# The head of a kernel's load queues, re-ordered: two thirds of DFT tables in front, small tables behind

## The chip, the cores and the metric

The kernel runs on one core of a Trainium2 chip. The metric is the device time of one execution in microseconds (us), the median of the runs that are shown; lower is better. The chip's engines named here are TensorE (PE; its weight loads are listed apart as PEld), VectorE (DVE), ScalarE (ACT), GpSimd (POOL) and SyncE (SP). Transfers are issued by SP, ACT and POOL and are carried by 16 DMA engines. The profile calls SP's queue q1, ACT's q10 and POOL's q0.

## What is computed

Two stages in a row. The first is a global filter along the sequence: a real FFT of length 3008 over each of 8 batches of 256 channels, a product with a complex filter, and the inverse FFT. The second is a small MLP on every one of the 24064 tokens, whose activation is "snake".

```python
X = np.fft.rfft(x, axis=1)                       # x: 8 x 3008 x 256
Y = X * (filt_r + 1j * filt_i)[None]             # 1505 x 256 filter
y = np.fft.irfft(Y, n=3008, axis=1)
h = y.reshape(24064, 256) @ w_in                 # 256 x 2048
s = np.sin(alpha * h)
out = (h + s * s / (alpha + 1e-9)) @ w_out       # 2048 x 256
```

All inputs and the output are float32 in DRAM. The kernel computes in float16 with float32 sums in PSUM.

## The kernel before, in words

**The transform.** 3008 is 47 x 64, so the FFT becomes two rounds of small DFTs as matmuls. The forward way is a 47-point DFT, then, with table `wb`, the 64-point part for each of 24 residues; the result `xs` is multiplied by the filter `fri` (`product`), and the backward way is `wg` (64-point part) and then `we` (47-point part). Tables `wb`, `wg` and `wgs` are 128 x 3072 float16 and are loaded in thirds of eight residues, 1024 columns, 256 KB each.

**Batch 0 is special.** For batches 1 to 7, each re-ordering between the rounds goes through DRAM (`scr`), beside the MLP of earlier tokens. Batch 0 has nothing to hide behind, so it stays on chip: `f1_chip(k)` for k = 0 to 7 (line 173) multiplies 94 rows of x by the table `wa2`; `turn1` (line 184) transposes with the identity `ident`; `f2x`, `product` and `g_chip` (line 194, with `wg` and `wgs`) follow; `turn2` transposes back; `f3` (line 281) uses `we2` for batch 0 and `we` for the others. `f1` (line 146, with `wq`) is the first round of batches 1 to 7.

**The MLP.** 47 chunks of 512 tokens. `mlp_in` (L310) makes 16 matmul pairs a chunk, ACT takes the sine (L312), DVE squares (L317), and `mlp_out` or `fast_out` (L329, L409) multiplies by `w_out`. From the first chunk on, the work of the transforms of batches 1 to 7 is dealt into the MLP by the slots of a written plan.

**The order at the start.** The program is written under a manual schedule: each engine executes its instructions in the order of the text. What matters here, in that order:

- SP issues `wa2` (94 rows of 192 bytes), `ident` (128 rows of 256 bytes) and the first third of `wb` (128 rows of 2 KB). ACT issues `alpha_r` (16 rows of 512 bytes), `ident32` (16 rows of 64 bytes), `we2` (96 rows of 188 bytes), `wq` (128 rows of 128 bytes) and `we` (96 rows of 188 bytes).
- POOL issues x of batch 0 in four parts of two transfers, 80 and 14 rows (`load_x(0, 4)`, line 133; a row is 8 KB in DRAM and 4 KB in SBUF), then by thirds: four transfers of the filter (`load_filter`, line 535), the rest of `wb` once, a third of `wg`, a third of `wgs`; then `w_in`, x of batch 1 and `w_out`. The first filter transfer is held by `gate` until the first half of x has landed. Completion semaphores are reused in turn, eight of them for POOL's transfers, so that a POOL transfer also waits for the one eight places before it.
- PE executes `prep_alpha` (line 481: a matmul of `alpha_r` and `ident32`), then `keep_busy(8, zero)` (line 529), eight 512-column matmuls of `ident` with zeros whose result nobody reads, then the eight `f1_chip`, with two more such matmuls after every second one, and then the list of steps at line 650.

In `prep_alpha` the wait is for `alpha_r` and `ident32`; in `keep_busy` for `ident`; in `f1_chip` for a part of x and for `wa2`. PE does none of them before the one ahead.

Of the kernel before, what the change touches and what calls it, by code (L numbers as in the profile page):

```python
# [67 lines left out]
def kernel(  # L68
# [10 lines left out]
    nc = tc.nc  # L79
# [3 lines left out]
    def dram(ap, off, dims):  # L83
# [3 lines left out]
    wq_d = nc.inline_tensor(wq_np, name="wq_tbl")  # L87
    wb_d = nc.inline_tensor(wb_np, name="wb_tbl")
    wg_d = nc.inline_tensor(wg_np, name="wg_tbl")
    we_d = nc.inline_tensor(we_np, name="we_tbl")  # L90
    wa2_d = nc.inline_tensor(wa2_np, name="wa2_tbl")
    we2_d = nc.inline_tensor(we2_np, name="we2_tbl")
    wgs_d = nc.inline_tensor(wgs_np, name="wgs_tbl")
    id32_d = nc.inline_tensor(np.eye(16).astype(np.float32), name="id32_tbl")
    id_d = nc.inline_tensor(np.eye(128).astype(np.float16), name="id_tbl")
# [17 lines left out]
    wq = cpool.tile([128, 64], FP16, name="wq")  # L113
    we = cpool.tile([4 * NK, GT], FP16, name="we")
    wa2 = cpool.tile([GT, 4 * NK], FP16, name="wa2")
    we2 = cpool.tile([4 * NK, GT], FP16, name="we2")
    wb = cpool.tile([128, NK * 128], FP16, name="wb")
    wg = cpool.tile([128, NK * 128], FP16, name="wg")
# [6 lines left out]
    xt, asb, scr1, bint, xs, z, t2, gsb, scr2, gin, yt, vt, po, ot, x_dma, w_in_dma, filter_dma, swap_dma = (  # L125
        {} for _ in range(18))

    def gate(ins, earlier):

        tc.add_manual_dep(ins.ins, earlier.ins.name, mybir.DependencyInfo(  # L130
            mybir.DependencyClass.Sync, mybir.DependencyReason.DATA), reason="order of transfers")

    def load_x(b, parts=2):

        xt[b] = (xbpool if b else vpool).tile([128 if b else GT, RP, C], FP16, name="xt", tag="xb" if b else "vt")
        n = RP // parts
        for h in range(parts):
            for p0, p1, row, step in (((0, 32, 0, R), (32, MT, 32 * R, R), (64, 96, RP, R), (96, 64 + MT, 32 * R + RP, R))
                                      if b else ((0, 80, 0, RP), (80, GT, 80 * RP, RP))):
                x_dma[b, h] = nc.gpsimd.dma_start(  # L140
                    out=xt[b][p0:p1, n * h:n * h + n, :],
                    in_=dram(x, (b * S + row + n * h) * C, [[step * C, p1 - p0], [1, n * C]]))
                if b > 2 and h == p0 == 0:
                    gate(x_dma[b, 0], swap_dma[b - 1, 5])
# [170 lines left out]
    def square(g, q):  # L315
        v4 = vt[g][:, 2 * q - 2:2 * q + 2, :]
        nc.vector.tensor_tensor(out=v4, in0=v4, in1=v4, op=ALU.mult)  # L317
# [156 lines left out]
    ident = cpool.tile([128, 128], FP16, name="ident")  # L474
# [6 lines left out]
    def prep_alpha():  # L481
        ps = out_bank("psal", 0)
        nc.tensor.matmul(out=ps[:, 0, 0:16], lhsT=alpha_r, rhs=ident32, start=True, stop=True)
        nc.vector.tensor_copy(out=alpha_t, in_=ps[:, 0, 0:16])
        nc.vector.tensor_scalar(out=recip, in0=alpha_t, scalar1=1e-9, scalar2=None, op0=ALU.add)
        nc.vector.reciprocal(out=recip, in_=recip)
# [124 lines left out]
        at(8 * g + 12.5, fast_mid, g)  # L611

    with tc.manual_schedule():
        nc.sync.dma_start(out=wa2, in_=wa2_d.ap())
        nc.sync.dma_start(out=ident, in_=id_d.ap())
        nc.scalar.dma_start(out=alpha_r, in_=moe_alpha.rearrange("(a p) -> a p", p=128))
        nc.scalar.dma_start(out=ident32, in_=id32_d.ap())
        nc.scalar.dma_start(out=we2, in_=we2_d.ap())
        nc.scalar.dma_start(out=wq, in_=wq_d.ap())
        nc.scalar.dma_start(out=we, in_=we_d.ap())  # L620
        nc.sync.dma_start(out=wb[:, 0:8 * 128], in_=wb_d.ap()[:, 0:8 * 128])
        zero = spool.tile([128, 512], FP16, name="zero", tag="z")
        nc.vector.memset(zero, 0.0)
        warm = cpool.tile([128, 1], FP32, name="warm")
        nc.vector.memset(warm, 0.0)
        nc.scalar.activation(out=warm, in_=warm, func=AFT.Sin)
        load_x(0, 4)
        wgs = ginpool.tile([128, NK * 128], FP16, name="wgs", tag="gin")
        for s0 in (0, 8, 16):
            cs = slice(128 * s0, 128 * s0 + 1024)  # L630
            load_filter(s0, 8, None if s0 else x_dma[0, 1])
            if s0 == 0:
                nc.gpsimd.dma_start(out=wb[:, 8 * 128:], in_=wb_d.ap()[:, 8 * 128:])
            nc.gpsimd.dma_start(out=wg[:, cs], in_=wg_d.ap()[:, cs])
            nc.gpsimd.dma_start(out=wgs[:, cs], in_=wgs_d.ap()[:, cs])
        for h in range(2):
            hs = slice(1024 * h, 1024 * h + 1024)
            for cb in range(2):
                w_in_dma[h, cb] = nc.gpsimd.dma_start(out=w_in16[:, cb, hs],
                                                      in_=moe_w_in[128 * cb:128 * cb + 128, hs])  # L640
        a_c = vpool.tile([128, 2, NK, 128], FP16, name="a_c", tag="vt")
        prep_alpha()
        keep_busy(8, zero)
        for k in range(8):
            f1_chip(k)
            if k % 2:
                keep_busy(2 if k < 7 else 1, zero)
        bint[0] = xbpool.tile([128, NK, C], FP16, name="bint", tag="xb")
        b_c = agpool.tile([128, 2, RP, NK, 4], FP16, name="b_c", tag="ag")
        for f, *args in (  # L650
                (keep_busy, 1, zero), (turn1, 0), (turn1, 1), (turn1, 2), (f2x, 0, 0), (f2x, 0, 1),
                (keep_busy, 1, zero), (turn1, 3), (turn1, 4), (fold_filter, 0, 0, 8), (turn1, 5), (f2x, 0, 2),
                (turn1, 6), (f2x, 0, 3), (fold_filter, 1, 0, 8), (turn1, 7), (product, 0, 0, 0), (product, 0, 0, 1),
                (product, 0, 1, 0), (f2x, 0, 4), (turn1, 8), (fold_filter, 0, 8, 8), (turn1, 9), (turn1, 10),
                (f2x, 0, 5), (keep_busy, 1, zero), (product, 0, 1, 1), (f2x, 0, 6), (fold_filter, 1, 8, 8),
                (f2x, 0, 7), (turn1, 11), (keep_busy, 2, zero), (g_chip, 0, 1), (f2x, 0, 8), (g_chip, 0, 0),
                (g_chip, 1, 1), (g_chip, 1, 0), (keep_busy, 1, zero), (product, 0, 2, 0), (product, 0, 2, 1),
                (keep_busy, 2, zero), (f2x, 0, 9), (keep_busy, 2, zero), (product, 0, 3, 0), (g_chip, 2, 0),
                (g_chip, 2, 1), (product, 0, 3, 1), (f2x, 0, 10), (fold_filter, 0, 16, 8), (f2x, 0, 11),
                (product, 0, 4, 0), (g_chip, 3, 1), (fold_filter, 1, 16, 4), (g_chip, 3, 0), (keep_busy, 2, zero),  # L660
                (fold_filter, 1, 20, 4), (product, 0, 4, 1), (keep_busy, 2, zero), (product, 0, 5, 0),
                (product, 0, 5, 1), (keep_busy, 1, zero), (g_chip, 4, 0), (g_chip, 4, 1), (g_chip, 5, 1, 2, 2),
                (g_chip, 5, 0), (g_chip, 5, 1, 0, 2, False), (keep_busy, 1, zero)):
            f(*args)
        gin[0] = ginpool.tile([4 * NK, RP, C], FP16, name="gin", tag="gin")
        for j in range(4):
            turn2(j)
        load_x(1, 4)
        load_w_out(0)
        load_w_out(1)  # L670
        for i in range(4):
            if i % 2 == 0:
                keep_busy(1, zero)
            f3(i // 2, i % 2)

        for g in range(NCH):
            fast_g = g - 1 in FAST
            for q in range(8):
                if g and q == 7 and not fast_g:
                    evict_out(g - 1, 0)  # L680
                mlp_in(g, 2 * q)
                if fast_g:
                    fast_out(g - 1, 16 * q, 16 * q + 8)
                elif g:
                    mlp_out(g - 1, q, 1)
                for f, args in plan.get(16 * g + 2 * q, ()):
                    f(*args)
                mlp_in(g, 2 * q + 1)
                if fast_g:
                    fast_out(g - 1, 16 * q + 8, 16 * q + 16)  # L690
                elif g:
                    mlp_out(g - 1, q, 0)
                for f, args in plan.get(16 * g + 2 * q + 1, ()):
                    f(*args)
                if g and q == 7:
                    if not fast_g:
                        evict_out(g - 1, 1)
                    store_out(g - 1, 0, 4, (nc.sync,))
                if q % 2:
                    square(g, q)  # L700
        out_last(NCH - 1)
# [28 lines left out]
```

## Time and profile before

| | us |
|---|---|
| median of 3 runs | 796.55 |
| lowest and highest | 796.06, 796.63 |
| the profiled execution | 796.66 |
| its span in the profile | 794.9 |
| PE busy | 779.0 (98%) |
| DVE busy | 682.5 (86%) |
| ACT busy | 652.8 (82%) |
| POOL busy | 53.7 (7%) |
| granted PE clock, mean | 0.999 |

The span is what the profiler saw from the first to the last instruction; the execution's time is 1.76 us longer. In a line of the timeline the first number is the start in us from the span's start, the second the time in us that the merged instructions took, then engine, line, operation, `output<-input`, the shape and the count; the bracket tells how long the engine was idle before and what ended that. The program's names are cut at the digits: `wa` is `wa2`, `ident` is `ident` or `ident32`, `we` is `we` or `we2`, and `w_in` also `w_in16` and others. In an answer on DMA, "packets" are the descriptors that the engines worked on, and a queue's "share of 16 engines" is the summed time of its packets by 16 times the window.

### The profile page before, as it was taken

How to read it: one execution, taken by the hardware profiler on the slowest of the kernel's cores; microseconds unless marked ns; L12 is line 12 of the kernel's file. 1: busy time of each engine (PE TensorE's matmuls, PEld its weight loads, DVE VectorE, ACT ScalarE, POOL GpSimd, SP SyncE). 2: the span in 40 equal slices, each digit the busy share in tenths (PEclk: the TensorE clock that was granted, in tenths of full speed). 3: DMA queues.
4: the chain of work that ended last, by engine and by line, in shares of the span. 5: the costliest groups of instructions: out<-in, count | busy, mean ns of one | idle time of the engine just before them, and what ended most of it. 6: DMA issues, size and time to landing. Idle time of an engine off the chain costs nothing.

```text
span 794.9 us, 20782 instructions
## 1 busy us (share of the span) xinstructions
PE 779.0 (98%) x8707; PEld 567.0 (71%) x8707; DVE 682.5 (86%) x851; ACT 652.8 (82%) x1290; POOL 53.7 (7%) x104
## 2 busy tenths in 40 slices
PE   7899999999999999999999999999999999999997
PEld 4657776777677776777767777777767777777776
DVE  4786988899889989899898988899988998888783
ACT  4897988898878988798888888889888898777773
POOL 5610020002000020000200020000200000000000
PEclk9999999999999999999999999999999999999999
DMA  9977368444862466633775348623675234321122
GB/s 194 187 127 249 110 158 182 130 115 108 195 176 76 124 144 150 175 92 90 165 158 160 81 111 205 165 77 94 150 192 163 81 107 110 65 54 28 28 55 54
DMA packets 74462, 101.08 MB, mean 127 GB/s; under 512 B 7896, under 2 KB 54760, under 8 KB 72856
## 3 DMA queue, kind: packets, MB, share of 16 engines
q1 hardware_dynamic: 65136, 78.39, 36.5%
q0 software_dynamic: 8704, 21.24, 14.0%
q8 instruction: 68, 1.11, 0.6%
q14 instruction: 26, 0.21, 0.1%
q10 hardware_dynamic: 528, 0.13, 0.1%
HBM read 59.62 MB, written 46.66 MB: 134 GB/s over the span
## 4 chain that ended last, share of the span: by engine, by line
PE 84%; DMA 4%; DVE 3%; issue 0%; SPq 0%; ACT 0%; ACTq 0%; DVEq 0%
PE ph L310 37%; PE pf L409 36%; PE psy L294 2%; PE psg L266 2%; PE psx L227 2%; PE po L329 2%; PE psa L159 1%; DMA w_in<-in_moe_w_in_dram 1%; DMA bint<-scr 1%; DMA out_dram<-ot 1%; PE pe L448 1%; DMA scr<-asb 1%; DVE t L252 1%; DVE vt L317 0%; DVE w_ina L526 0%; DVE asb L163 0%
## 5 line engine op out<-in xcount | busy, mean ns | idle before, releaser
L312 ACT ACTIVATE vt<-ph 128x512 f16<-128x512 f32 x688 | 410.4, 604 | 93.4 <-PE ph L310 82.5
L310 PE MATMUL ph<-yt,w_ina 128*128 128x512 f16 x1376 | 409.6, 379 | 0.0
L317 DVE TENSOR_TENSOR vt<-vt 128x2048 f16<-128x2048 f16 x188 | 229.4, 1220 | 38.7 <-ACT vt L312 38.3
L409 PEld LDWEIGHTS <-s 128*128 128x128 f16 x2688 | 179.8, 98 | 79.6
L409 PEld LDWEIGHTS <-vt 128*128 128x128 f16 x2016 | 135.4, 98 | 59.6 <-DVE ot L423 0.4
L409 PE MATMUL pf<-tb,s 128*128 128x128 f16 x2016 | 153.6, 219 | 0.0
L423 DVE TENSOR_TENSOR ot<-pf,ot 128x512 f32<-128x512 f32 (+1 forms) x168 | 93.3, 555 | 30.6 <-PE pf L409 28.7
L310 PEld LDWEIGHTS <-w_ina 128*128 128x128 f16 x1376 | 107.1, 98 | 12.4 <-issue 9.9
L409 PE MATMUL pf<-w_out,vt 128*128 128x128 f16 x1344 | 109.3, 219 | 0.0
L360 DVE TENSOR_TENSOR s<-vt 128x2048 f16<-128x2048 f16 x84 | 102.5, 1220 | 0.9
L140 POOL DMA_DIRECT2D xt<-in_x_dram x72 | 36.8, 519 | 463.2 <-PE ph L310 267.1
L409 PEld LDWEIGHTS <-yt 128*128 128x128 f16 x672 | 47.9, 98 | 20.0
L231 ACT CAST xs<-psx 128x512 f16<-128x512 f32 x94 | 55.8, 599 | 3.7 <-PE psx L227 0.9
L409 PE MATMUL pf<-w_out,s 128*128 128x128 f16 x672 | 58.1, 219 | 0.0
L268 ACT CAST gsb<-psg 128x512 f16<-128x512 f32 x84 | 49.5, 589 | 4.5 <-PE psg L266 0.2
L360 DVE TENSOR_TENSOR s<-s,vt 128x2048 f16<-128x2048 f16 x42 | 51.3, 1222 | 0.9
L409 PE MATMUL pf<-tb,vt 128*128 128x128 f16 x672 | 51.2, 219 | 0.0
L360 DVE TENSOR_TENSOR s<-vt,s 128x2048 f16<-128x2048 f16 x42 | 51.1, 1217 | 0.0
L312 ACT ACTIVATE vt<-ph,alpha_t 128x512 f16<-128x512 f32 x64 | 43.8, 708 | 8.2 <-PE ph L310 8.1
L409 PE MATMUL pf<-m_t,yt 128*128 128x128 f16 x504 | 48.6, 219 | 0.0
L296 ACT CAST yt<-psy 128x376 f16<-128x376 f32 (+45 forms) x126 | 46.1, 366 | 1.5
L294 PE MATMUL psy<-we,gin 96*128 96x94 f16 x512 | 42.3, 204 | 0.0
(91 smaller groups left out, 702.3 us busy)
## 6 DMA issues: line engine op xcount, KB each, us to landing
scr<-asb SPq DMA_DIRECT2D x56, 192.0 KB
bint<-scr SPq DMA_DIRECT2D x21, 512.0 KB
scr<-gsb SPq DMA_DIRECT2D x21, 512.0 KB
out_dram<-ot SPq DMA_DIRECT2D x31, 320.0 KB
t<-xs SPq DMA_DIRECT2D x72, 128.0 KB
xt<-in_x_dram POOLq DMA_DIRECT2D x24, 256.0 KB, 7.1
gin<-scr SPq DMA_DIRECT2D x7, 768.0 KB
out_dram<-ot SPq DMA_DIRECT2D x16, 256.0 KB
```

What stands on the lines that cost most here:

```text
L140: x_dma[b, h] = nc.gpsimd.dma_start(out=xt[b][p0:p1, n * h:n * h + n, :], in_=dram(x, (b * S + row + n * h) * C, [[step * C, p1 - p0], [1, ...
L227: nc.tensor.matmul(out=ps[:, i, :], lhsT=wb[:, 128 * (2 * t + i):128 * (2 * t + i) + 128], rhs=bint[b][:, 2 * t + i, :], start=True, stop= ...
L231: (nc.vector.tensor_copy if b == 0 and t in (4, 5) else nc.scalar.copy)(out=xs[b, t // 2][:, t % 2 * 2:t % 2 * 2 + 2, :], in_=ps)
L268: nc.scalar.copy(out=gsb[b][:, 2 * t:2 * t + 2, :], in_=ps)
L294: nc.tensor.matmul(out=ps[:, t, :], lhsT=gin[b][:, 4 * a + t, 128 * cb:128 * cb + 128], rhs=we if b else we2, start=True, stop=True)
L296: (nc.vector.tensor_copy if G < 2 and cb == 0 else nc.scalar.copy)(out=yt[g][:, cb, :, lo:lo + n], in_=ps[:, :, 0:n])
L310: nc.tensor.matmul(out=ph, lhsT=(w_in16 if g < 4 else w_ina)[:, cb, 128 * jb:128 * jb + 128], rhs=yt[g][:, cb], start=(cb == 0), stop=(cb ...
L312: nc.scalar.activation(out=vt[g][:, jb, :], in_=ph, func=AFT.Sin, scale=alpha_t[:, jb:jb + 1] if g < 4 else 1.0)
L317: nc.vector.tensor_tensor(out=v4, in0=v4, in1=v4, op=ALU.mult)
L360: nc.vector.tensor_tensor(out=o, in0=a, in1=b, op=op)
L409: nc.tensor.matmul(out=ps[:, part, i], lhsT=a, rhs=b, start=first, stop=last)
L423: add = lambda out, in0, in1: nc.vector.tensor_tensor(out=out, in0=in0, in1=in1, op=ALU.add)
```

## The change

The first third of `wb` and the first third of `wg` become SP's first two transfers. `ident` and `wa2` move from SP to the head of ACT's queue, in this order, ahead of `alpha_r` and `ident32`. `we2`, `wq` and `we` move from ACT to SP, behind a gate on the last transfer of the second filter third (`filter_dma[8, 1]`). The first third of `wg` leaves POOL's queue; everything behind it on POOL is one place earlier. No arithmetic instruction changes or moves on PE, DVE or ACT.

```diff
     with tc.manual_schedule():
-        nc.sync.dma_start(out=wa2, in_=wa2_d.ap())
-        nc.sync.dma_start(out=ident, in_=id_d.ap())
+        nc.sync.dma_start(out=wb[:, 0:8 * 128], in_=wb_d.ap()[:, 0:8 * 128])
+        nc.sync.dma_start(out=wg[:, 0:8 * 128], in_=wg_d.ap()[:, 0:8 * 128])
+        nc.scalar.dma_start(out=ident, in_=id_d.ap())
+        nc.scalar.dma_start(out=wa2, in_=wa2_d.ap())
         nc.scalar.dma_start(out=alpha_r, in_=moe_alpha.rearrange("(a p) -> a p", p=128))
         nc.scalar.dma_start(out=ident32, in_=id32_d.ap())
-        nc.scalar.dma_start(out=we2, in_=we2_d.ap())
-        nc.scalar.dma_start(out=wq, in_=wq_d.ap())
-        nc.scalar.dma_start(out=we, in_=we_d.ap())
-        nc.sync.dma_start(out=wb[:, 0:8 * 128], in_=wb_d.ap()[:, 0:8 * 128])
...
             load_filter(s0, 8, None if s0 else x_dma[0, 1])
             if s0 == 0:
                 nc.gpsimd.dma_start(out=wb[:, 8 * 128:], in_=wb_d.ap()[:, 8 * 128:])
-            nc.gpsimd.dma_start(out=wg[:, cs], in_=wg_d.ap()[:, cs])
+            if s0:
+                nc.gpsimd.dma_start(out=wg[:, cs], in_=wg_d.ap()[:, cs])
             nc.gpsimd.dma_start(out=wgs[:, cs], in_=wgs_d.ap()[:, cs])
...
+        for tab, src in ((we2, we2_d), (wq, wq_d), (we, we_d)):
+            gate(nc.sync.dma_start(out=tab, in_=src.ap()), filter_dma[8, 1])
```

## The prediction, made before the changed kernel was run

> **What bounds the kernel now.** I read the page first.
>
> ```profile
> PE 779.0 (98%) x8707; PEld 567.0 (71%) x8707; DVE 682.5 (86%) x851; ACT 652.8 (82%) x1290; POOL 53.7 (7%) x104
> PE 84%; DMA 4%; DVE 3%; issue 0%; SPq 0%; ACT 0%; ACTq 0%; DVEq 0%
> ```
>
> PE is busy for 98% and carries 84% of the chain that ended last. So what is lost or won before the MLP starts (first `mlp_in` at 35.84) moves the end by as much: behind it PE has nearly no idle time to give back. The change touches only the first 36 us, so I read those in the timeline.
>
> ```profile
> 3.18 0.50 PEld L483 LDWEIGHTS psal<-ident,alpha_r 16*128 16x128 f32 x2 [3.18 <-DMA alpha_r<-in_moe_alpha_dram]
> 3.21 0.57 PE L483 MATMUL psal<-ident,alpha_r 16*128 16x16 f32 x2 [3.21 <-DMA ident<-id_tbl]
> 3.72 3.59 PE L533 MATMUL idle<-zero,ident 128*128 128x512 f16 x8
> ...
> 7.40 1.19 PEld L178 LDWEIGHTS <-xt 94*128 94x128 f16 x16 [1.00 <-DMA xt<-in_x_dram]
> 7.44 1.31 PE L178 MATMUL psa<-wa,xt 94*128 94x96 f16 x16
> ...
> 9.60 0.84 PE L178 MATMUL psa<-wa,xt 94*128 94x96 f16 x16 [0.42 <-DMA xt<-in_x_dram]
> ...
> 11.29 0.84 PE L178 MATMUL psa<-wa,xt 94*128 94x96 f16 x16 [0.41 <-DMA xt<-in_x_dram]
> ...
> 13.15 0.84 PE L178 MATMUL psa<-wa,xt 94*128 94x96 f16 x16 [0.59 <-DMA xt<-in_x_dram]
> ...
> 21.84 0.69 DVE L548 COPY fri<-fri 64x2048 f16<-64x2048 f16 x1 [0.49 <-DMA fri<-in_filt_r_dram]
> ```
>
> Two things to see. PE waits for the four parts of x up to 13.15; from then to 36 us DVE and ACT are the busy ones, and only one wait of theirs is for a load, the 0.49 at 21.84. And everything on PE stands behind the 16x16 matmul of L483: it starts when `alpha_r` and `ident32` have landed, the eight idle matmuls follow, and the first `f1_chip` starts 4.23 us after it (7.44 - 3.21).
>
> Then the DMA answer for four windows, in this order: 1.6 to 2.6 us (nothing was moved before 1.6), 2.6 to 3.1, 4.5 to 5.1, 6.6 to 7.4. Behind a queue's name stand its packets, their MB, and their time as a share of 16 engines.
>
> ```profile
> q1 hardware_dynamic: 240, 0.05, 23.7%
> q10 hardware_dynamic: 64, 0.01, 5.3%
> ```
> ```profile
> q0 software_dynamic: 14, 0.06, 164.0%
> ```
> ```profile
> q0 software_dynamic: 21, 0.09, 73.3%
> q1 hardware_dynamic: 22, 0.05, 22.0%
> q10 hardware_dynamic: 20, 0.00, 3.1%
> ```
> ```profile
> q0 software_dynamic: 39, 0.16, 95.8%
> q10 hardware_dynamic: 46, 0.01, 9.1%
> ```
>
> Three readings:
>
> - By 2.6 q1 has moved 240 packets: 94 rows of `wa2`, 128 of `ident`, and 18 others. Each engine that takes part in a transfer adds one small closing packet. `ident` makes 16, so `wa2` makes 2: its 94 rows (2 x 47) ran on two engines, 47 each. q10's 64 are 32 rows of `alpha_r` and `ident32` and 32 closings, so those ran on all 16.
> - Before 2.6 no packet of x moves. From 2.6 to 3.1 nothing but x moves: 14 packets, 1.64 x 16 x 0.5 / 14 = 0.94 us each.
> - After that the queues take turns packet by packet, whatever the size: 21, 22 and 20 with three queues (a turn of all three lasts 16 x 0.6 / 21 = 0.46 us), 39 to 46 with two (0.33 us). A 188-byte row of a small table gets one turn for each 8 KB row of x.
>
> **The change part by part.**
>
> *`wa2`, `alpha_r`, `ident32`.* Before, all are through by 2.6, ahead of x. After, ACT issues `ident`, `wa2`, `alpha_r`, `ident32` about 0.45 apart (its four issues before took 0.39 to 0.45), from 0.73, while SP puts 2 KB rows on every engine. A 2 KB packet takes 22.0% x 16 x 0.6 / 22 = 0.096 us. On the two engines of `wa2`, `ident` has 8 rows and a closing; taking turns with `wb`, 9 x (0.096 + 0.018) is 1.0 us from the first packets at 1.6 to 1.7 (0.018: an `ident` row, 23.7% x 16 x 1.0 / 240, rounded up). That is 2.6 to 2.7: x is there, and `wa2` has not begun. From then the pair of engines owes q10 47 + 1 turns for `wa2`, and 2 each for `alpha_r` and `ident32`, which I take to stand behind it in the same queue: 52 turns. x and its closings are only some 32 packets an engine; the filter's rows follow.
>
> When has q0 given an engine 52 turns? In the DMA answer from 2.6 to 13.5 us q0 has 831 packets, 52 for each of 16 engines. That is with 23 turns of q10 beside them (368 packets in the same window); the 29 more cost 9.1% x 16 x 0.8 / 46 = 0.025 each, 0.7 together. So `ident32` lands at 14.2 (13.5 if they cost nothing, 15.0 if x's first packets on the pair are slow ones again). From the last packet before (by 2.6) to the matmul (3.2) pass 0.6: L483 starts at 14.8, bounds 14.0 and 15.6. That is 11.6 later than 3.2.
>
> *What of it is given back.* At 14.8 + 4.23 = 19.0 all x has landed, so the waits between the four parts vanish: 0.42 + 0.41 + 0.59 = 1.42 by PE's rows, 0.88 + 0.88 + 1.05 = 2.81 by its weight loads; I take the middle, 2.1, since DVE's evictions (1.02 per part) and PE's own idle pairs (0.6) keep their pace. The 0.49 at 21.84 vanishes too (0.47 with the gap that remains); no other wait up to 36 us is for a load. Sum: 11.6 - 2.1 - 0.5 = +9.0.
>
> *First third of `wb` at the head; `wg` with it.* Needed at 15.33 and 22.27, landed by about 7 us (`wb`'s nine turns an engine by 2.7, then 0.94 and eight turns of 0.46 for `wg`'s): no gain of their own. `wg` leaves POOL's queue: 0.57 of issue and 128 x 0.096 / 16 = 0.77 of all engines, earlier for everything behind it. Only the 0.49 wait could use that, and it is counted.
>
> *`we2`, `wq`, `we` on SP behind the gate.* The gate opens when the second filter third has landed, issued at 15.38, 5.7 median to landing: about 21. SP has nothing else to issue until `scr<-asb` (its longest wait is 49.4). `we2` is needed at 34.51 and now 9 later, `wq` at 45.77: 13 us of cover; without it each us late would be a us. x loses 20 packets an engine of q10's: 4.1% of 9.8 us, 0.40, while `wg` replaces `wb` in its way.
>
> *The queues' heads.* SP's two issues take 0.43 each instead of three of 0.32 to 0.43, ACT's four instead of five: ACT's table load (3.05) comes 0.45 earlier, and ACT is idle up to 7.95. Nothing.
>
> *POOL later.* x of batch 1 waits for the PE's release of its buffer (28.09) and moves by the 9 us; `w_in` will then have landed, so the 5.1 us that POOL waits for it vanish, and no engine waits there. Its first use (45.77) moves by the same 9.
>
> The profiled execution took 796.66, 1.76 over its span, 0.11 over the median: 796.66 + 9.0 = 805.7 there, 805.6 as a median. Bounds of this case: 14.0 with 2.81 and 0.49 back gives +7.5, 804.1; 15.6 with 1.42 back gives +11.0, 807.5.
>
> **The rivals.**
>
> 1. *A turn takes many small rows.* Were a turn to take a group of `wa2`'s rows, between 8 (an engine's share of `ident`) and all 47, these need 1 to 6 turns and the whole debt is 6 to 11. 2.6 + 0.94 + 5 to 10 turns of 0.46 is 5.8 to 8.1; L483 starts at 6.4 to 8.7; 3.2 to 5.5 late, less 2.1 and 0.5: +0.6 to +2.9, 797.2 to 799.5. Against it: 21, 22 and 20, where q10's rows had 188 bytes, close to `wa2`'s 192. For it: 46 against 39, where q10 got more. The Trainium skill (DMA: Bandwidth & Descriptors, "Queues, rings and completion order") states such a rule: an engine drains a whole packet of some 9 to 17 descriptors from one queue before it turns to the next; by that, as an estimate, 3 to 6 turns and 798.1 to 799.5. The counts of this trace, one for one, disagree with it.
>
> 2. *The small tables get through in time, and the head of the queue pays: faster.* The place is L483. It decides at 5.3 (3.2 plus the 2.1 of slack in x's waits): with `ident32`, `alpha_r` and `wa2` landed by 4.7, nothing is lost, and 0.47 at 21.84 and 0.40 of x are won: 795.7. For it: the engines are nearly idle before 2.6 (5.3% + 23.7%). Against it: ACT's second issue can start only near 1.15, and 47 rows need 0.6 even alone.
>
> 3. *`alpha_r` and `ident32` pass `wa2`* (or part of the queue does). Then the eight idle matmuls run while `wa2` lands at 14.1, and `f1_chip` starts at 14.7 instead of 7.4: 7.3 - 2.6 = +4.7, 801.3.
>
> 4. *The pair of engines does worse*, the later filter rows in the way as well: past 808.5.
>
> **How the numbers follow.** Forecast 0.76, rival 1 0.08, rival 2 0.08, rival 3 0.05, rival 4 0.03. The measurement can tell about 0.2%, 1.6 us, from no change: up to 795.0 is faster, to 798.1 the same. Rival 2 with its 0.9 counts as the same, with a quarter of its chance kept for more than 1.6; a third of rival 1 (0.03) lies there too. Faster 0.02, same 0.09, slower 0.89. The range reaches from rival 3 with a margin, 800.5, to 808.5: 0.81.
>
> **What would show it.** Right: L483 near 14.8, ended by a DMA; `f1_chip` near 19.0, its four groups without waits for x; no idle time before DVE's copy of the second filter third; first `mlp_in` near 44.8, and the same 9 us at every later stage. q1's early packets without `wa2`, and q10 still moving 192-byte rows after 10 us. Wrong: L483 before 8 (turns are not packets, or `wa2` is spread over 16 engines); or a late L483 with an early end, if PE's later stages have slack that the page does not show.

## The result, and the profile after

| us | before | after |
|---|---|---|
| median of 16 runs each, same chip | 797.57 | 798.90 |
| lowest and highest | 796.06, 798.57 | 797.75, 801.22 |
| the profiled execution, its span | 796.66, 794.9 | 798.97, 797.2 |

The changed kernel is slower by a ratio of 1.0021, 95% interval [1.0012, 1.0030]: 1.0 to 2.4 us, 1.7 in the middle (the two medians alone differ by 1.33). The forecast was 9.0 us, and its range began at 800.5. From the page of the changed kernel:

```profile
PE 777.7 (98%) x8707; PEld 566.8 (71%) x8707; DVE 682.6 (86%) x851; ACT 652.8 (82%) x1290; POOL 52.7 (7%) x103
PE 86%; DMA 2%; DVE 2%; ACT 0%; issue 0%; ACTq 0%; DVEq 0%
```

PE is busy for 1.3 us less than before (779.0), so the loss is time in which PE waits. The timeline shows where (start, time taken, engine, line, operation, and in the bracket the idle time and what ended it):

```profile
0.73 0.38 ACTq L616 DMA_DIRECT2D ident<-id_tbl  x1
1.14 0.54 ACTq L617 DMA_DIRECT2D wa<-wa_tbl  x1
1.71 0.47 ACTq L618 DMA_DIRECT2D alpha_r<-in_moe_alpha_dram  x1
2.21 0.44 ACTq L619 DMA_DIRECT2D ident<-id_tbl  x1
...
8.38 0.58 PE L483 MATMUL psal<-ident,alpha_r 16*128 16x16 f32 x2 [8.38 <-DMA ident<-id_tbl]
8.89 3.30 PE L533 MATMUL idle<-zero,ident 128*128 128x512 f16 x8
...
12.03 0.84 PE L178 MATMUL psa<-wa,xt 94*128 94x96 f16 x16
...
15.38 0.84 PE L178 MATMUL psa<-wa,xt 94*128 94x96 f16 x16
...
23.68 0.69 DVE L548 COPY fri<-fri 64x2048 f16<-64x2048 f16 x1
...
38.57 0.69 ACT L312 ACTIVATE vt<-ph,alpha_t 128x512 f16<-128x512 f32 x1 [0.20 <-PE ph L310]
```

Read against before: L483 starts at 8.38 instead of 3.21, 5.17 late. The last `f1_chip` pair starts at 15.38 instead of 13.15, 2.23 late: the waits for x are gone, and PE takes 7.00 us from L483 to there instead of 9.94. DVE's copy of the second filter third is 1.84 late, without the wait of 0.49. The first sine of the MLP is 1.75 late (36.82 before). From there the two executions run nearly in parallel: the sines move apart by 0.65 more at 236 us, where PE waits 0.8 for `bint<-scr`, and together by 0.28 at 305; the span ends 2.3 later.

L483 is still late because of a DMA. But it is not the one that I named. In the DMA answer for 2.6 to 3.1 us, then for 4.5 to 5.1 (packets, MB, share of 16 engines):

```profile
q1 hardware_dynamic: 88, 0.15, 84.1%
q10 hardware_dynamic: 114, 0.02, 23.2%
```
```profile
q0 software_dynamic: 27, 0.11, 88.3%
q10 hardware_dynamic: 3, 0.00, 0.9%
```

In the first window, where I had x alone, x does not move at all, and q10 moves 114 packets: the end of `ident` and the begin of `wa2`, whose rows lie between 2.94 and 4.21 in the packet records of the trace, and x's first packet is at 3.50 instead of 2.61. In the second window x moves 27 packets and q10 only 3, although `alpha_r` was issued at 1.71. The first row of `alpha_r` moves at 5.02, the last closing packet of `ident32` at 7.80, and L483 follows 0.6 later.

### The profile page after: what moved, and what is told of

Same layout as the page of the kernel before. It is cut to its first block, busy times and chain, and to the rows that moved or that the text cites. A ratio compares the mean times of both kernels' runs of the same rounds, so it can differ in the third digit from the quotient of the medians.

```text
span 797.2 us, 20781 instructions
## 1 busy us (share of the span) xinstructions
PE 777.7 (98%) x8707; PEld 566.8 (71%) x8707; DVE 682.6 (86%) x851; ACT 652.8 (82%) x1290; POOL 52.7 (7%) x103
## 4 chain that ended last, share of the span: by engine, by line
PE 86%; DMA 2%; DVE 2%; ACT 0%; issue 0%; ACTq 0%; DVEq 0%
PE ph L310 38%; PE pf L409 37%; PE psy L294 2%; PE psg L266 2%; PE psx L227 2%; PE po L329 2%; PE psa L159 2%; DMA w_in<-in_moe_w_in_dram 1%; DMA bint<-scr 1%; PE pe L448 1%; DVE t L252 1%; DVE w_ina L526 0%; DVE vt L317 0%; DVE z L257 0%; DMA out_dram<-ot 0%; DVE ot L459 0%
```

## The experiments

Every ratio is to runs of the kernel before on the same chip. The expectations speak of these theories: **A**, `alpha_r` and `ident32` are held back by `wa2`'s 47 rows on its pair of engines; **B**, they are late by themselves, as ACT's third and fourth transfers, issued when x is about to begin; **C**, they are late because of the two thirds of tables at the head of SP's queue.

### First set: what holds L483, and is it the loss? (before 796.62)

**e1, `alpha_r` and `ident32` first on ACT, `wa2` last.**

```diff
+        nc.scalar.dma_start(out=alpha_r, in_=moe_alpha.rearrange("(a p) -> a p", p=128))
+        nc.scalar.dma_start(out=ident32, in_=id32_d.ap())
         nc.scalar.dma_start(out=ident, in_=id_d.ap())
         nc.scalar.dma_start(out=wa2, in_=wa2_d.ap())
-        nc.scalar.dma_start(out=alpha_r, in_=moe_alpha.rearrange("(a p) -> a p", p=128))
-        nc.scalar.dma_start(out=ident32, in_=id32_d.ap())
```

> Of the changed kernel, only ACT's first four transfers are put in another order: alpha_r, ident32, ident, wa2. Theory A (what stands behind wa2's 47 rows on two engines is held back on all engines): alpha_r and ident32 land by 2.6 us, L483 starts near 3.2, ident and wa2 land by 5, the idle matmuls start within 1 us of L483, the first f1_chip near 7.4 as before; the time 0.4 to 0.9 under the kernel before, 2.2 to 2.8 under the changed one. Theory B (whatever ACT issues after about 1.6 us gets its turn only when an engine's five rows of the first part of x are through, whatever stands ahead of it): L483 near 3.2 too, but ident, now issued at 1.6, lands at 5.5 to 7.5, the idle matmuls start at 6 to 8 and the first f1_chip at 9.5 to 11.5; the time between the two kernels.

Measured: 798.52, ratio 1.0036 [1.0022, 1.0050]. Its timeline:

```profile
4.08 0.57 PE L483 MATMUL psal<-ident,alpha_r 16*128 16x16 f32 x2 [4.08 <-DMA ident<-id_tbl]
...
7.35 3.59 PE L533 MATMUL idle<-zero,ident 128*128 128x512 f16 x8 [2.70 <-DMA ident<-id_tbl]
...
13.22 1.44 PE L178 MATMUL psa<-wa,xt 94*128 94x96 f16 x16 [2.28 <-DMA fri<-in_filt_r_dram]
```

L483 is early and the lateness has moved to `wa2`. The bracket of the last line names a filter transfer, but POOL's queue is not what PE reads here: `wa2`'s last row ends at 12.58, and PE starts 0.6 later. This is the forecast's mechanism beside x. From 6.35 us on, the last 26 rows take 19 turns of one row or two, one turn per 0.33 us, which is the length of one 4 KB packet of x (329 ns mean). The DMA answer from 6.6 to 12.5:

```profile
q0 software_dynamic: 429, 1.18, 103.8%
q10 hardware_dynamic: 28, 0.01, 0.7%
```

The rows ahead of these went by in bursts at 5.2 to 6.1, 12 ns apart on an engine, while q0 kept only 10 to 14 of the 16 engines busy. So whoever stands fourth on ACT does get caught beside x; in the changed kernel `wa2` stands second and does not. The profiled execution (803.77) was the slowest of 11, so its 13.22 stands at the late end. Not all of its loss is `wa2`: behind that wait the first three `f1_chip` groups took 1.44 to 1.49 instead of 0.84 (more on this pace at the end), so that 6.36 us passed from the first group to the last, for 3.35 in the changed kernel.

**e2, `wa2` in two transfers** of 80 and 14 rows, so that the 80 spread over all engines.

```diff
-        nc.scalar.dma_start(out=wa2, in_=wa2_d.ap())
+        nc.scalar.dma_start(out=wa2[0:80], in_=wa2_d.ap()[0:80])
+        nc.scalar.dma_start(out=wa2[80:GT], in_=wa2_d.ap()[80:GT])
```

> Of the changed kernel, only the load of wa2 is cut into rows 0 to 79 and 80 to 93, on ACT in its place; by the counting of closing packets this spreads it from 2 engines over 16 and 14. Theory A: nothing is held back any more, L483 starts at 3.7 to 4.7, the first f1_chip by 8.5, and the time falls by 1.5 to 2.5 under the changed kernel. Theory B: alpha_r and ident32 are now ACT's fourth and fifth transfers, issued at 2.2 and 2.7, and land no earlier than in the changed kernel: L483 at 7 to 9, the time unchanged within 1.

Measured: 799.29, ratio 1.0038 [1.0026, 1.0050].

```profile
2.32 0.47 ACTq L619 DMA_DIRECT2D alpha_r<-in_moe_alpha_dram  x1
...
8.54 0.57 PE L483 MATMUL psal<-ident,alpha_r 16*128 16x16 f32 x2 [8.54 <-DMA ident<-id_tbl]
```

With no pair of engines owing 47 rows, L483 is as late as before the edit (8.54 against 8.38), and `alpha_r`, issued 0.61 later, starts at 5.35. Theory A falls, B stands.

**e3, `prep_alpha()` moved** from ahead of `keep_busy(8, zero)` to behind the `f1_chip` loop.

```diff
-        prep_alpha()
         keep_busy(8, zero)
...
+        prep_alpha()
```

> Of the changed kernel, only the matmul of alpha_r and ident32 with its three DVE steps is moved behind the eight f1_chip; the transfers stay as they are. If the late L483 at the head of PE's queue is the whole of the loss (both theories), the idle matmuls start when ident has landed, near 3.7, the first f1_chip near 7.4 to 8, the fourth group waits for x again near 13.1, and the time falls by 1.5 to 2.5 under the changed kernel, less up to 0.6 for the three DVE steps, which now stand ahead of the first transposes' evictions. The rival (x itself lands later in the changed kernel, and L483 only hides it): the fourth group starts at 14 or later and less than 1 is won.

Measured: 796.90, ratio 1.0006 [0.9996, 1.0016].

```profile
3.87 3.27 PE L533 MATMUL idle<-zero,ident 128*128 128x512 f16 x8 [3.87 <-DMA ident<-id_tbl]
7.00 0.84 PE L178 MATMUL psa<-wa,xt 94*128 94x96 f16 x16
...
12.57 0.84 PE L178 MATMUL psa<-wa,xt 94*128 94x96 f16 x16 [0.60 <-DMA xt<-in_x_dram]
...
13.55 0.39 PE L483 MATMUL psal<-ident,alpha_r 16*128 16x16 f32 x2
```

All DMAs are those of the changed kernel. When nothing stands behind L483, the loss can no longer be told from none, `f1_chip` starts earlier than in the kernel before, the waits for x are back, and x itself ends 0.6 earlier (12.57 against 13.15). That the three late tables, which take no turns from x here, are the reason is not shown: with them late, the last part of x was waited for until 12.31 to 12.57 in e3, e7, e11 and e12, but until 13.07 in e9.

**e4, small tables at both heads:** SP issues `wa2`, `ident`, then the two thirds; ACT issues `alpha_r` and `ident32`.

```diff
+        nc.sync.dma_start(out=wa2, in_=wa2_d.ap())
+        nc.sync.dma_start(out=ident, in_=id_d.ap())
         nc.sync.dma_start(out=wb[:, 0:8 * 128], in_=wb_d.ap()[:, 0:8 * 128])
         nc.sync.dma_start(out=wg[:, 0:8 * 128], in_=wg_d.ap()[:, 0:8 * 128])
-        nc.scalar.dma_start(out=ident, in_=id_d.ap())
-        nc.scalar.dma_start(out=wa2, in_=wa2_d.ap())
```

> Of the changed kernel, wa2 and ident are put back to the head of SP's queue, wb's and wg's thirds behind them; alpha_r and ident32 lead ACT's. So it is the kernel before with the first third of wg moved from POOL to SP and the three small tables late. Both theories: L483 at 3.2, the first f1_chip at 7.4; DVE's wait of 0.49 before the copy of the second filter third is gone, x is earlier by up to 0.4; the time 0.4 to 0.9 under the kernel before. If wg beside x costs more than the three tables did, the fourth part of x lands after 13.5 and the time is the kernel before's or above it.

Measured: 797.75, ratio 1.0018 [1.0009, 1.0027].

```profile
7.92 1.44 PE L178 MATMUL psa<-wa,xt 94*128 94x96 f16 x16 [0.61 <-DMA xt<-in_x_dram]
```

L483 is at 3.21, yet the first `f1_chip` waits 0.61 for x, which now shares the engines with 512 KB of tables. In the profile that is made up by the filter (first sine at 36.46, 0.36 earlier than before), while the median is 1.1 later. The profiled execution lost its time behind the start-up: from the first sine to the end it took 759.5, the longest of all 14 profiles (757.7 to 759.5; 758.1 in before), with a wait of 1.2 instead of 0.3 for `bint<-scr` at 329 us among others. Such waits differ from one execution to the next, and whether this edit causes them is open. So this kernel loses as much as the changed one without a late L483: an L483 on time is not enough for no loss.

### Second set: which part of the change does it? (before 796.45)

**e6, the first third of `wg` back on POOL**, all else as changed.

```diff
-        nc.sync.dma_start(out=wg[:, 0:8 * 128], in_=wg_d.ap()[:, 0:8 * 128])
...
-            if s0:
-                nc.gpsimd.dma_start(out=wg[:, cs], in_=wg_d.ap()[:, cs])
+            nc.gpsimd.dma_start(out=wg[:, cs], in_=wg_d.ap()[:, cs])
```

> Of the changed kernel, the first third of wg goes back to POOL, behind the rest of wb; SP's head is then the first third of wb alone. In the changed kernel x's first packets began at 3.5 us, when SP's rows were through, and wa2 used the time before them. If it is SP's 512 KB that holds x back, x now begins at 2.6 to 3.0, wa2's 47 rows on each of two engines are caught behind it, one for each row of x, and land at 8 to 14: the first f1_chip at 10 to 14 in the profiled execution, the time 2 to 6 over the kernel before and over the changed kernel, although less stands in the way. If x still begins near 3.5, wa2 lands near 4.2 again, L483 near 8.4, and the time is the changed kernel's within 1.

Measured: 798.18, ratio 1.0022 [1.0011, 1.0032].

```profile
7.61 0.57 PE L483 MATMUL psal<-ident,alpha_r 16*128 16x16 f32 x2 [7.61 <-DMA ident<-id_tbl]
```

x's first packet is at 2.70, but `wa2` was not caught behind it, as I had expected for that case: its rows ran at 2.93 to 3.73. So `wg` on SP accounts for x's later begin, and for at most 0.77 of the 5.17 us by which L483 is late (0.48 against e13, the second profile of the changed kernel).

**e7, the late tables alone:** the kernel before, with `we2`, `wq` and `we` on SP behind the gate.

> The kernel before with one part of the change alone: we2, wq and we move from ACT to SP behind the gate. Nothing else moves. The small tables took 4.1% of the 16 engines over 9.8 us, 0.40 us of x's way: the four x groups at 7.4, 9.3, 11.0 and 12.8 or up to 0.4 earlier than before, DVE's 0.49 wait at 21.84 unchanged or smaller; the time 0 to 0.6 under the kernel before. If the tables rode in gaps that x leaves, the time is the kernel before's. Slower only if the gate on SP costs something that no row shows.

Measured: 796.71, ratio 0.9996 [0.9987, 1.0006]: no cost and no gain that can be measured, as the cover of 13 us had said.

**e8, the kernel before with `alpha_r` and `ident32` third and fourth on ACT.** No big table moves.

```diff
+        nc.scalar.dma_start(out=we2, in_=we2_d.ap())
+        nc.scalar.dma_start(out=wq, in_=wq_d.ap())
         nc.scalar.dma_start(out=alpha_r, in_=moe_alpha.rearrange("(a p) -> a p", p=128))
         nc.scalar.dma_start(out=ident32, in_=id32_d.ap())
-        nc.scalar.dma_start(out=we2, in_=we2_d.ap())
-        nc.scalar.dma_start(out=wq, in_=wq_d.ap())
         nc.scalar.dma_start(out=we, in_=we_d.ap())
```

> The kernel before with ACT's order alone changed: we2, wq, then alpha_r, ident32, then we. SP's head stays wa2, ident, wb; nothing of 47 rows on two engines is on ACT's queue. Theory B (a transfer that ACT issues after about 1.6 us gets its turn only after x's first rows): alpha_r and ident32, issued at 1.6 and 2.1, land at 5 to 7, L483 starts at 5.5 to 7.5, the first f1_chip at 9.7 to 11.7, the time 0.3 to 2 over the kernel before. Theory C (it is SP's 512 KB at the head that held them up): L483 at 3.3 to 4.5 and the time within 0.5 of the kernel before's.

Measured: 798.54, ratio 1.0024 [1.0013, 1.0035].

```profile
1.60 0.46 ACTq L618 DMA_DIRECT2D alpha_r<-in_moe_alpha_dram  x1
2.09 0.44 ACTq L619 DMA_DIRECT2D ident<-id_tbl  x1
```
```profile
7.53 0.58 PE L483 MATMUL psal<-ident,alpha_r 16*128 16x16 f32 x2 [7.53 <-DMA ident<-id_tbl]
```

Two places on a queue, 0.87 us of issue, and L483 is 4.3 late. This swap alone costs what the whole change costs. Theory C falls as the main cause.

**e9, e7 with the first third of `wb` on POOL right behind x.**

```diff
-        nc.sync.dma_start(out=wb[:, 0:8 * 128], in_=wb_d.ap()[:, 0:8 * 128])
...
         load_x(0, 4)
+        nc.gpsimd.dma_start(out=wb[:, 0:8 * 128], in_=wb_d.ap()[:, 0:8 * 128])
```

> A version that may beat both: the kernel before with the three small tables late, as in the run before last, and the first third of wb moved from SP to POOL, right behind the four parts of x. x then has the engines to itself: 0.8 (wb) and 0.4 (tables) come out of its way, the four groups at 7.4, 9.0, 10.6 and 12.0, and wb lands by 14, when the first f2x needs it (15.3 before, 14.2 now). The time 0.7 to 1.3 under the kernel before. If wb lands after 14.2, f2x waits for it and all is given back.

Measured: 796.28, ratio 1.0002 [0.9988, 1.0015]. With no table beside it, x ended no earlier than in before (its last part was waited for until 13.07, where I had expected 12.0). Why is open.

### Third set: is x what makes them late? (before 796.50)

**e10, the changed kernel with x held until `ident32` has landed.** The edit adds two lines ahead of L178 and L483, which are L180 and L485 here.

```diff
+                if b == h == p0 == 0:
+                    gate(x_dma[0, 0], small_dma)
...
-        nc.scalar.dma_start(out=ident32, in_=id32_d.ap())
+        small_dma = nc.scalar.dma_start(out=ident32, in_=id32_d.ap())
```

> The changed kernel, but POOL issues x of batch 0 only when ident32 has landed. Theory (alpha_r and ident32 come late because their rows take turns with x's long packets, and x is given the first of them): without x beside them, and with wa2 through about 1.2 us after its first row, alpha_r and ident32 are through by 3.5 to 4.2 and the 16x16 matmul of L483 starts at 4.0 to 4.8, not at 8.4. x then begins at about 4.8 to 5.5 instead of 3.5, its last part is waited for at about 14.6 to 15.3, the waits between its parts are back, and the first sine is 1.0 to 2.0 later than before: 797.5 to 799. Rival (a third or fourth transfer on ACT's queue is slow whatever runs beside it): L483 stays at 7 to 8.5, x begins at about 9, first sine 5 or more later: above 801.

Measured: 801.24, ratio 1.0050 [1.0036, 1.0063].

```profile
5.40 0.57 PE L485 MATMUL psal<-ident,alpha_r 16*128 16x16 f32 x2 [5.40 <-DMA ident<-id_tbl]
5.56 4.31 POOL L140 DMA_DIRECT2D xt<-in_x_dram  x8 [5.11 <-DMA ident<-id_tbl]
```

Without x, the first row of `alpha_r` moves at 3.50, beside the last rows of `wa2`, and all four small tables are through by 4.43. So x is worth 2.98 of the 5.17 us; the other 2.19 come from the queue as it now stands (later issue, 512 KB and `wa2` beside or ahead, which this run does not tell apart). The mechanism of B holds, but I had L483 at 4.0 to 4.8 and not 5.40, and x begins at 6.92, not by 5.5. What is lost here is no longer L483: PE waits 0.78 and 0.54 for x, and its matmuls stay at the slow pace to the end of the fourth group, so that 7.05 us pass from the first `f1_chip` to the last, for 3.35 in the changed kernel. What the hold would cost at the faster pace is not shown.

**e11, e7 with the first third of `wg` on SP too, held until x has landed.**

```diff
-            nc.gpsimd.dma_start(out=wg[:, cs], in_=wg_d.ap()[:, cs])
+            if s0:
+                nc.gpsimd.dma_start(out=wg[:, cs], in_=wg_d.ap()[:, cs])
...
+        gate(nc.sync.dma_start(out=wg[:, 0:8 * 128], in_=wg_d.ap()[:, 0:8 * 128]), x_dma[0, 3])
```

> The kernel before with the three small tables late on SP (as in the run of that part alone) and the first third of wg on SP too, held until the last part of x has landed. If the start-up is set by x and then by the second filter third: x's last part is waited for at about 12.5 (before 13.15), the second filter third comes 0.6 or more earlier than with wg ahead of it on POOL, so that DVE's copy starts at 21.2 to 21.4 (before 21.84), and the first sine is 0.6 to 1.1 earlier than in the kernel before: 795.4 to 796.2 against 796.5. Rival: the second filter third is bound by what the DMA engines have to move and not by its place on POOL's queue: the wait there stays at 0.5 to 1.5, the first sine is within 0.5 of before, and the time within 0.1%.

Measured: 796.54, ratio 1.0002 [0.9988, 1.0015].

```profile
35.49 0.69 ACT L312 ACTIVATE vt<-ph,alpha_t 128x512 f16<-128x512 f32 x1 [0.20 <-PE ph L310]
```

Its profile was more than I had expected, with the copy at 20.55 and the first sine 1.33 earlier than before; its median was not.

### Fourth set: the same kernels again (before 796.40)

**e12, e11 unedited.**

> The kernel of the run before (small tables late, first third of wg on SP behind x) once more, on another occasion, for a second profile and more times. Theory (its start-up is shorter each time, and waits for transfers later in the kernel scatter by more than that): first sine again 35.3 to 36.0 (36.8 in the profile of before), L483 at 3.1 to 3.3, the last part of x at 12.2 to 12.6; median 0 to 1.2 under that of before. Rival (the start-up itself scatters by 1 us or more from one execution to the next, and the first profile was a lucky one): first sine at 36.3 or later.

Measured: 796.75, ratio 1.0003 [0.9992, 1.0013]. The copy of the second filter third and the first sine this time:

```profile
21.59 0.69 DVE L548 COPY fri<-fri 64x2048 f16<-64x2048 f16 x1 [0.96 <-DMA fri<-in_filt_r_dram]
```
```profile
36.49 0.69 ACT L312 ACTIVATE vt<-ph,alpha_t 128x512 f16<-128x512 f32 x1 [0.20 <-PE ph L310]
```

The rival holds: the start-up of one and the same kernel moves by 1.0 us between two executions, and most of that is whether the second filter third is waited for. No version here beats the kernel before by more than its measurement can tell.

**e13, the changed kernel unedited.**

> The changed kernel once more, unedited, for a second profile. Theory (alpha_r and ident32 come late each time): L483 at 7.5 to 9, the first f1_chip 11 to 12.7, first sine 1.0 to 2.3 later than in the profile of before (37.8 to 39.1), ratio 1.001 to 1.003. Rival (the first profile's late L483 was an accident of one execution): L483 under 7 or over 10, first sine less than 1.0 later.

Measured: 797.99, ratio 1.0018 [1.0005, 1.0030].

```profile
8.09 0.58 PE L483 MATMUL psal<-ident,alpha_r 16*128 16x16 f32 x2 [8.09 <-DMA ident<-id_tbl]
8.60 3.59 PE L533 MATMUL idle<-zero,ident 128*128 128x512 f16 x8
11.98 1.49 PE L178 MATMUL psa<-wa,xt 94*128 94x96 f16 x16
```

The late L483 comes back within 0.3. The first sine, at 39.29, is 0.7 later than in the first profile and just outside what I had expected. The difference is PE's own pace: the idle matmuls took 3.59 instead of 3.30, the first `f1_chip` group 1.49 instead of 0.84, and from L483 to the last group PE needed 8.02 us instead of 7.00.

## Why the prediction was wrong, and where it was right

- **What bounds the kernel: right.** L483 is the instruction that decides, it came late because of a DMA, everything on PE followed, and the loss went through to the end. In e3 it disappears when L483 is taken out of the way. The runs with a late L483 in PE's way (e2, e6, e8, e13) lose a ratio of 1.0018 to 1.0038; with L483 out of the way or on time, e3, e7, e9, e11 and e12 stay between 0.9996 and 1.0006. e4 is the exception, with 1.0018 and L483 on time; e1 and e10 lose by other waits.
- **The wrong step: "By 2.6 ... x is there, and `wa2` has not begun".** I took x's begin (2.6) from the trace of before as if it stood by itself. With 512 KB at SP's head x's first packet came at 3.50, and `wa2` had moved 63 of its 94 rows by then. With 256 KB there (e6) x began at 2.70, and `wa2` still got through, at 2.93 to 3.73; fourth on ACT (e1) it did not. So its place on ACT's queue is what saves it.
- **The second wrong step: "which I take to stand behind it in the same queue: 52 turns".** In the changed kernel `wa2` had ended at 4.21, ahead of the first row of `alpha_r`, and spreading it (e2) changed nothing. `alpha_r` and `ident32` were late on their own account, which no rival of mine had as its cause. The lateness was 8.38 - 3.21 = 5.17 us and not 11.6.
- **Turns of one row: right, but only while another queue has work for the engine.** In the changed kernel 59 rows of `wa2` ran between 2.94 and 3.38, 12 ns apart on each of two engines. Then the start times show the turns: from 3.19 on one engine and from 3.39 on the other, eight 2 KB packets of SP, each beginning 12 ns after one row of `wa2`, most turns 0.092 us long; behind the eighth the rows are 12 ns apart again. Eight is an engine's share of `wg`'s 128 rows, so the stretch before was one in which SP had nothing for these two engines. In e3 and e13 the rows of `wa2` change to steps of 0.092 in the same way. So the forecast had the price of a turn right and took for granted that SP's rows and then x would be beside `wa2` all the time. The Trainium skill (DMA: Bandwidth & Descriptors, "Queues, rings and completion order") gives some 9 to 17 descriptors for a turn; the turns that can be followed here, beside SP and beside x in e1, have one row or two.
- **What is given back: right in size, in part by luck.** Predicted 2.1 for x (1.42 to 2.81), measured 5.17 - 2.23 = 2.94 at the last `f1_chip`, and 9.94 - 8.02 = 1.92 in e13. The 1.02 between these two profiles of one kernel is PE's pace, for which the forecast had no term. Predicted 0.47 for the filter, measured 2.23 - 1.84 = 0.39. The same formula with L483 at 8.38 gives 5.17 - 2.1 - 0.47 = +2.6, against +2.3 in the span and +1.7 by the ratio. So the term that was mis-sized is the lateness.
- **Rival 1** gave the right times (797.2 to 799.5, L483 at 6.4 to 8.7) by luck: its turns of many rows did not occur, and `wa2`'s rows were not what L483 waited for. **Rival 3** (801.3) had the two tables pass `wa2`; they did not.
- **The late tables: right.** e7 found nothing, and in the changed kernel SP issues them at 22.11 to 22.96, without a wait for them further on.

## What to carry to other kernels

Of an in-order engine's first wait, ask which transfers it needs and what place these have on their queue. Here 9 KB (16 rows of 512 bytes and 16 of 64) came 4 to 5 us later, and cost 1.7, for standing third and fourth instead of first and second, where they met a large load; the order of a few small issues was enough for that (e8), with no big table moved. When a change to one queue moves the load that was to collide with another queue's, work out anew when that load begins. Turns cost a small transfer only where the other queue has rows for the same engine at that moment. And a start-up that one profile shows 1 us shorter may not be: profile it twice.

## What the runs showed of the hardware that I had not expected

- **On ACT's queue, a transfer that has not begun when x begins waits, whether it was issued at 1.6 or at 2.3.** The first row of the third or later transfer on ACT came 1.41 us after x's first packet in before (`we2`, issued at 1.63), 1.55 in e8, 1.65 in e6, 1.52 in the changed kernel and e3, 1.53 in e13, and 1.80 in e2 (`alpha_r`, issued at 1.6 to 2.3); in e1 it was 0.91 (`ident`, issued at 1.63). With x held (e10) `alpha_r`'s first row moved at 3.50 instead of 5.02. Between 4.5 and 5.1 us in the changed kernel x moved 27 packets and q10 3, all three at the end: the turns had hardly begun. It is not a fixed number of x's rows, since 24 (e8) to 86 (e2) packets of x had begun by that first row. And it does not hold for SP: `wb`, third there and issued at 1.51, moved its first row 0.58 us after x's first packet in before and 0.70 in e8. Why the first turn on ACT comes so late was not settled.
- **The closings count.** In e6 the last data row of `ident32` ended at 5.96, but the last closing packet of q10 began at 7.13, and L483 started at 7.61. Beside x a 4-byte packet can come 1.2 us behind the data.
- **PE starts at half its later pace.** The idle matmuls start 0.43 us apart at first and 0.22 apart later, and an `f1_chip` group takes 1.49 or 0.84, with the granted clock at 1.0 in the mean. In 11 of the 14 profiles the change came some 3 to 5 us after the first idle matmul. In e4, e1 and e10, where PE waited 0.6, 2.3 and 0.8 us behind the idle matmuls, it came 8.0, 12.3 and 12.5 us after it. So a wait of PE in the start-up may cost more than its own length; what sets the moment of the change was not tested.
